# Attention into a mixture of experts on one core: other row order for the first w1 load, a longer hand-kept emission order

## The chip, the cores and the metric

One Trainium2 chip, one of its NeuronCores. The core has TensorE (PE), VectorE (DVE), ScalarE (ACT), GpSimd (POOL), a queue that only issues transfers (SP), and sixteen DMA engines. The metric is device time in microseconds of one launch; "before" was run three times. Times inside the launch are from one profiled execution and count from its first instruction.

## What is computed

Linear attention over 8 batches, 8 heads, 576 positions and 64 features, then a mixture of 8 experts over the 4608 tokens, every expert for every token, weighted by a matrix P that eight rounds of row and column normalising give.

```python
def _attn_ref(q, k, v):
    def phi(x):
        return np.where(x > 0, x, np.exp(x) - 1.0) + 1.0
    q_p, k_p = (phi(q), phi(k))
    kv = np.einsum('bhsd,bhse->bhde', k_p, v)
    z = np.sum(k_p, axis=2)
    num = np.einsum('bhsd,bhde->bhse', q_p, kv)
    den = np.einsum('bhsd,bhd->bhs', q_p, z)[..., None] + 1e-06
    return (num / den).astype(np.float32)

def _moe_ref(x, w_gate, w1, w2):           # x: 4608 x 512, w1: 8 x 512 x 1024, w2: 8 x 1024 x 512
    logits = x @ w_gate
    logits = logits - logits.max()
    P = np.exp(logits)
    for _ in range(8):
        P /= P.sum(1, keepdims=True) + 1e-09
        P /= P.sum(0, keepdims=True) + 1e-09
        P *= N / E
    for e in range(E):
        h = np.maximum(x @ w1[e], 0.0)
        ye = h @ w2[e]
        out += P[:, e:e + 1] * ye
```

## The kernel before

**Tiling.** The attention runs in 16 pairs (batch b, half g of the heads: two rows of two heads each). A pair loads k, q and v, makes phi(k) and phi(q) (exp on ACT, add-and-max and min on DVE), multiplies k with v (`kv_ps`), transposes q on TensorE (`att`), and forms denominators (`att`) and numerators (`num_ps`); the quotient goes to `xT`, the transposed input of the experts, in fp16. The experts run in units of 512 tokens, nine to an expert (g = 0 to 8). The first five units of expert 0 are plain products: layer 1 (`hq`, eight blocks of 128 hidden features) and layer 2 (`ye`). All later units but the very last use a seven-product scheme of Strassen's kind in both layers. It needs sums of blocks of w1 (tile W, four DVE instructions an expert), of w2 (tile T, four more), of x (kept in `xd` in HBM and loaded again as `xs` for each unit) and of h (tile S).

**How the order comes about.** Nothing is emitted in program order. Every piece of work is added to a plan (`_Plan.add`) with an engine, a cost in microseconds, dependencies and buffers, and gets a running number. `run` then emits the pieces one at a time: first those of the list `_FRONT`, in exactly its order, and after its end by its own rule, which takes whatever the cost figures say can start first. The engines execute what was emitted for them in that order, each its own queue, so the list fixes each queue. An entry is the number and a letter for the engine: p PE, a ACT, d DVE, g POOL, s SP, m a transfer's landing, n nothing (an allocation). The costs steer only the plan; no instruction depends on them.

**Numbers used in this document.** 2 to 47: small products that keep TensorE busy at the start. 48: k of pair 0 (on SP). 50, 52: q and v of pair 0 (POOL). 76, 78, 80: k, q, v of pair 1; 126, 128, 130 those of pair 2; 154, 156, 158 those of pair 3; 182, 184, 186 those of pair 4; 210, 212, 214 those of pair 5. 104 and 106: the two halves of w_gate. 109, 111, 114, 116: the four pieces of expert 0's w1, all on POOL; 120 and 123: the two halves of its w2. 600 to 603: layer 1 of the first unit for four blocks of hidden features, first half of the contraction (chunks 0 and 1 of four); 604, 606, 608, 610: the second half; 612 to 618 the other four blocks; 620 to 627 its layer 2. 985 and up: expert 1, 57 numbers to a unit, so 1156 to 1212 is its fourth. 1499 and 1501: the two loads of expert 2's w1; 1505: that of its w2; 1508 to 1511: the four sums W of expert 2; 1512 to 1515: the four sums T.

**The weight loads.** `load_w` allocates the tile and issues one POOL transfer for each entry of `pieces`; the fp32 weights are cast to fp16 on the way. The tile of w1 has 128 rows, four chunks and 1024 columns; row p of chunk c holds feature 256 * (p // 64) + 64 * c + p % 64 of x. `load_w1` with `parts=2` is used once, for expert 0. A product of the first half of the contraction depends on the first two pieces, one of the second half on the last two. All other w1 loads are two transfers of 64 rows and all four chunks. Eight POOL transfers can be in flight: the ninth is issued when the first has landed.

## Time and profile before

| | us |
|---|---|
| median of 3 runs | 979.66 (978.38 to 979.71) |
| the profiled execution | 979.93 |
| its span, first to last instruction | 978.2 |
| TensorE busy in the span | 956.6 |
| TensorE busy 0 to 10, 10 to 20, 20 to 30 | 8.67, 8.06, 2.15 |
| TensorE busy 30 to 40, 40 to 50 | 10.00, 9.99 |
| TensorE busy 260 to 280 | 17.07 |
| granted clock, 20 to 30 and 30 to 40 | 0.73, 0.76 |
| granted clock, 260 to 280; mean of the run | 0.91; 0.992 |

"Busy" counts an engine's instructions, overlaps once. Matmuls are pipelined: one of 512 columns is recorded as 0.379 us long, but the next starts 0.215 us after it, so a stretch of many is measured from start to start. The page's rows of busy shares have 40 slices of 24.5 us; the granted clock is TensorE's, as a share of full speed. In the lists of waits a row has the waiting engine, what it waited for, the total, how often, and the longest. A transfer's time to landing runs from its issue to its last mark.

Rows of the start, start time and length first (PE's small products left out):

```
7.82 1.16 ACT L422 ACTIVATE eq<-qin 128x1152 f16<-128x1152 f16 x1 [1.85 <-DMA qin<-in_q_dram]
9.97 0.85 POOL L289 DMA_DIRECT2D w<-in_moe_w_dram x1
19.04 0.75 DVE L473 TENSOR_TENSOR xT<-num_ps,rden 128x576 f16<-128x576 f32 x1
20.86 0.68 PE L414 MATMUL att<-ident,tq 128*128 128x128 f16 x9
29.69 1.04 PE L646 MATMUL hq<-xT,w 128*128 128x512 f16 x2 [7.00 <-DMA w<-in_moe_w_dram]
44.57 1.89 PE L874 MATMUL ye<-w,h 128*128 128x512 f16 x8
```

### The profile page before, as it was taken

Reading aid. Unit: us, or ns where it says so; the run is one execution under the profiler, and the core shown is the slowest. Engines: PE = TensorE matmul, PEld = TensorE weight load, DVE = VectorE, ACT = ScalarE, POOL = GpSimd, SP = SyncE. Lnnn points to the kernel's source line nnn. Section 1 sums busy time; section 2 is a strip of 40 time slices with the busy share of each in tenths; the row PEclk is TensorE's granted clock in tenths of the full one; section 3 lists DMA queues with packets and bytes.
Section 4 is the critical chain, followed back from the end, with each engine's and each line's share of the span. In section 5 each row is a group of like instructions: output and inputs, shape, how many; then the busy total and the mean of one; then the engine's idle time right before and its main releaser. Section 6 shows DMA issues by size and latency. Waiting matters only on the chain.

```text
span 978.2 us, 20907 instructions
## 1 busy us (share of the span) xinstructions
PE 956.6 (98%) x8480; PEld 796.8 (81%) x8480; DVE 775.9 (79%) x1489; ACT 569.8 (58%) x1012; POOL 147.1 (15%) x209
## 2 busy tenths in 40 slices
PE   7799999999899999999999999999999999999998
PEld 3365566678788888888888888888888888888886
DVE  6598988788778788878888788878888788877775
ACT  6598854466555555555555555555555555555553
POOL 6343200001212111121112111121112111111110
PEclk9799999999999999999999999999999999999999
DMA  9997927122625422272225422272224422236554
GB/s 196 221 228 176 183 93 233 37 76 76 125 76 122 116 76 77 76 162 77 77 76 125 114 77 76 77 162 76 76 77 123 116 76 76 77 91 168 163 163 108
DMA packets 49264, 112.51 MB, mean 115 GB/s; under 512 B 7952, under 2 KB 29200, under 8 KB 49168
## 3 DMA queue, kind: packets, MB, share of 16 engines
q1 hardware_dynamic: 21056, 75.57, 23.6%
q0 software_dynamic: 27712, 35.09, 19.6%
q8 instruction: 66, 1.08, 0.4%
q10 hardware_dynamic: 400, 0.52, 0.2%
q14 instruction: 30, 0.25, 0.1%
HBM read 119.69 MB, written 17.69 MB: 140 GB/s over the span
## 4 chain that ended last, share of the span: by engine, by line
PE 91%; DMA 4%; DVE 3%; ACT 1%; issue 1%; POOL 0%; DVEq 0%; ACTq 0%; POOLq 0%
PE ye L992 33%; PE hq L768 23%; PE att L768 12%; PE ye L874 6%; PE Zye L768 6%; PE Zye L992 5%; DMA w<-in_moe_w_dram 3%; PE hq L646 3%; PE att L445 1%; PE kv_ps L388 1%; PE num_ps L445 1%; DMA qin<-in_q_dram 1%; DVE xT L473 0%; PE att L414 0%; PE att L489 0%
## 5 line engine op out<-in xcount | busy, mean ns | idle before, releaser
L1006 DVE SCALAR_TENSOR_TENSOR acc<-ye,P_sb,acc 128x256 f32<-128x256 f32 x620 | 267.6, 479 | 125.2 <-PE ye L992 124.5
L768 PEld LDWEIGHTS <-W 128*128 128x128 f16 x2144 | 209.8, 98 | 34.0 <-issue 6.4
L992 PEld LDWEIGHTS <-S 128*128 128x128 f16 x1984 | 194.1, 98 | 22.4
L1016 POOL TENSOR_TENSOR acc<-acc,st 128x256 f32<-128x256 f32 x124 | 87.6, 726 | 720.2 <-ACT st L1013 720.2
L992 PE MATMUL ye<-T,S 128*128 128x256 f16 x1488 | 192.8, 273 | 0.0
L768 PEld LDWEIGHTS <-w 128*128 128x128 f16 x1608 | 157.6, 98 | 21.6 <-issue 0.5
L800 ACT ACTIVATE h<-hq 128x512 f16<-128x512 f32 x134 | 80.0, 597 | 142.3 <-PE hq L768 137.7
L992 PEld LDWEIGHTS <-h 128*128 128x128 f16 x1488 | 146.0, 98 | 17.5 <-issue 0.3
L768 PE MATMUL att<-xs,W 128*128 128x256 f16 x1008 | 151.6, 273 | 4.2 <-DVE h L803 3.8
L768 PE MATMUL hq<-xs,W 128*128 128x256 f16 x1008 | 151.2, 273 | 0.4 <-ACT Zye L780 0.4
L768 PE MATMUL hq<-xs,w 128*128 128x256 f16 x1008 | 141.2, 273 | 0.3 <-DVE h L803 0.3
L797 ACT ACTIVATE h<-Zye 128x512 f16<-128x512 f32 x134 | 80.1, 598 | 45.7 <-PE Zye L768 44.7
L1013 ACT ACTIVATE st<-Zye,P_sb 128x256 f32<-128x256 f32 x124 | 52.3, 471 | 75.7 <-PE Zye L992 75.5
L803 DVE CUSTOM_DVE_ANT_0 h<-att,s 128x512 f16<-128x512 f32 x126 | 86.5, 686 | 11.1 <-ACT s L787 10.2
L787 ACT COPY s<-hq 128x512 f32<-128x512 f32 x126 | 73.5, 583 | 35.9 <-PE hq L768 35.7
L965 DVE TENSOR_TENSOR S<-h 128x1024 f16<-128x1024 f16 x124 | 85.2, 687 | 11.3 <-ACT h L800 11.2
L780 ACT COPY Zye<-hq 128x512 f32<-128x512 f32 x134 | 77.8, 581 | 27.7 <-PE hq L768 27.6
L803 DVE CUSTOM_DVE_ANT_0 h<-hq,s 128x512 f16<-128x512 f32 x126 | 86.6, 687 | 3.2 <-PE hq L768 2.7
L794 ACT COPY s<-att 128x512 f32<-128x512 f32 x126 | 74.5, 591 | 5.3 <-PE att L768 3.3
L874 PE MATMUL ye<-w,h 128*128 128x512 f16 x312 | 77.1, 379 | 0.0
L768 PE MATMUL Zye<-xs,w 128*128 128x256 f16 x504 | 75.6, 273 | 0.0
L992 PE MATMUL ye<-T,h 128*128 128x256 f16 x496 | 65.2, 275 | 0.0
(104 smaller groups left out, 958.8 us busy)
## 6 DMA issues: line engine op xcount, KB each, us to landing
xs<-xd SPq DMA_DIRECT2D x63, 896.0 KB, 4.6
kin<-in_k_dram POOLq DMA_DIRECT2D x15, 576.0 KB, 6.5
out_dram<-acc SPq DMA_DIRECT2D x67, 128.0 KB, 2.4
w<-in_moe_w_dram POOLq DMA_DIRECT2D x16, 512.0 KB, 9.3
w<-in_moe_w_dram POOLq DMA_DIRECT2D x7, 1024.0 KB, 13.2
qin<-in_q_dram POOLq DMA_DIRECT2D x16, 288.0 KB, 7.1
vv<-in_v_dram POOLq DMA_DIRECT2D x16, 288.0 KB, 6.4
xd<-acc SPq DMA_DIRECT2D x5, 512.0 KB, 2.7
```

The costliest lines, as they stand in the source:

```text
L768: nc.tensor.matmul(dst[:, p, :], lhsT=lhs(p, c), rhs=rhs(c), start=(first and p == 0 and c == 0), stop=(c == 1), skip_group_check=True)
L780: nc.scalar.copy(out=Zt[1], in_=gX["tile"])
L787: nc.scalar.copy(out=gs2["tile"], in_=gX["tile"])
L794: nc.scalar.copy(out=gs5["tile"], in_=gR["tile"])
L797: nc.scalar.activation(out=hd(0, 0), in_=Zt[1], func=AF.Relu)
L800: nc.scalar.activation(out=hd(1, 0), in_=gX["tile"], func=AF.Relu)
L803: nc.vector._custom_dve(TENSOR_ADD_SAT, out=dst, in0=ps, in1=sb, s0=3.0e38, s1=0.0)
L874: nc.tensor.matmul(gy[tt]["tile"], lhsT=gh["tile"][:, f, ds(P * tt, P)], rhs=gw2["tile"][:, f, :], start=(f == 0), stop=(f == NFT - 1))
L965: nc.vector.tensor_tensor(out=Sx[:, i], in0=a0, in1=a1, op=op)
L992: nc.tensor.matmul(bank(g_)[:, s, :], lhsT=lhs(s, kk), rhs=rhs(kk), start=(new and s == 0 and kk == 0), stop=(kk == 3), skip_group_check=True)
L1006: nc.vector.scalar_tensor_tensor(out=dst(), in0=bank(g_)[:, s, :], scalar=P_sb[:, gg, e:e + 1], in1=dst(), op0=ALU.mult, op1=ALU.add)
L1016: nc.gpsimd.tensor_tensor(out=dst(), in0=dst(), in1=gst["tile"], op=ALU.add)
```

## The change

Three things change. Expert 0's w1 is still loaded in four pieces of 256 KB, but a piece was all 128 rows of one chunk, with the two groups of 64 rows as the outermost dimension on the HBM side; it becomes 64 rows of two chunks, with the 64 rows outermost on both sides. The first two pieces still hold chunks 0 and 1 and the last two chunks 2 and 3, so what depends on which pair stays. The list `_FRONT` is replaced: it had 1236 entries and ended in expert 1's sixth unit (1275p); it has 1465 and ends in expert 1's last unit. And two cost figures of the plan change: a piece's transfer from 1.4 to 1.6, and the add-and-max of phi(q) from 0.5 to 0.455.

```diff
-    1n 106g 107m 108n 119n 599n 48s 49m 2p 3p 50g 51m 4p 0g 5p 6p 52g 53m 7p 8p 76g 77m 9p 78g 79m 10p 11p 54a 55d
-    80g 81m 12p 13p 14p 15p 128g 129m 16p 56d 17p 18p 126g 127m 19p 20p 21p 61n 22p 62a 63d 130g 131m 23p 24p 25p 26p
-    27p 64d 156g 157m 28p 29p 30p 31p 32p 57n 109g 110m 58p 65p 59d 111g 112m 33p 60a 66d 34p 83d 67p 89n 82a 114g
...
-    1232p 1206d 1231a 1207p 1233a 1229a 1236p 1209d 1238p 1208d 1237a 1234p 1199a 1240p 1235a 1200g 1273p 1241d 1275p
+    1n 108n 119n 599n 109g 110m 48s 49m 2p 3p 50g 51m 4p 0g 5p 6p 52g 53m 7p 8p 76g 77m 9p 78g 79m 10p 11p 80g 81m
+    12p 13p 14p 15p 126g 127m 16p 54a 55d 17p 18p 128g 129m 19p 20p 21p 22p 130g 131m 23p 24p 25p 26p 27p 61n 111g
+    112m 62a 63d 28p 29p 56d 30p 31p 32p 33p 64d 34p 35p 36p 37p 57n 156g 157m 58p 65p 59a 82a 114g 115m 38p 66d 39p
...
+    104g 105m 122n 622p 200d 194a 617a 180p 201p 181d 620p 202a 178p 203p 125n 179d 244g 245m 621p 204a 623p 628d
+    106g 107m 217d 637p 639p 223n 216a 218d 270g 271m 224a 624p 225d 205a 226d 219n 272g 273m 220p 640d 638a 227p
...
+    549p 948p 550d 962p 949a 551d 912p 922d 635a 958p 913p 631a 959d 1498n 1499g 1500m 963a 988p 1501g 1502m 920d
...
+    1386n 1312g 1393p 1325d 1357a 1441s 1442m 1395p 1394a 1314g 1358d 1391p 1362p 1505g 1506m 1359d 1364p 1360d 1363a
...
+    1447a 1512d 1370a 1413p 1383d 1443n 1371g 1450p 1410d 1414a 1516s 1517m 1452p 1382d 1448p 1415d 1419p 1416d 1421p
+    1420a 1417d 1451a 1424p 1418d 1423d 1454p 1427a 1422d 1429p 1449a 1455d 1428g 1432p 1430d 1431d 1456p 1453d 1458p
...
-                ts_.append(add(("dma", (1.4 if nm == "w1" and len(pieces) > 1 else 2.75)), lambda _: None, deps=[ti],
+                ts_.append(add(("dma", (1.6 if nm == "w1" and len(pieces) > 1 else 2.75)), lambda _: None, deps=[ti],
...
-            return load_w(moe_w1, "w1", p_w1, [[((slice(None), c), PW * F * c, [[256 * F, 2], [F, PW], [1, F]])
-                                                for c in (2 * i, 2 * i + 1)] for i in range(2)], e, shape=[P, NDT, F], **kw)
+            return load_w(moe_w1, "w1", p_w1, [[((slice(64 * r, 64 * r + 64), slice(2 * i, 2 * i + 2)),
+                                                 256 * F * r + 2 * PW * F * i, [[F, PW], [PW * F, 2], [1, F]]) for r in range(2)]
+                                               for i in range(2)], e, shape=[P, NDT, F], **kw)
...
-        t3 = fadd(("dve", 0.5), f_qm, deps=[t0], use=[gin["q"], gtq], prio=pr)
+        t3 = fadd(("dve", 0.455), f_qm, deps=[t0], use=[gin["q"], gtq], prio=pr)
```

The queue of POOL at the start, before: 106, 50, (identity), 52, 76, 78, 80, 128, 126, 130, 156, 109, 111, 114, 116, 154, 158, 182, 186, 184, 120, 123, 210, 212, 214. After: 109, 50, (identity), 52, 76, 78, 80, 126, 128, 130, 111, 156, 114, 116, 154, 158, 182, 184, 186, 120, 123, 210, 212, 214, 240, 242, 268, 104, 244, 106.

## The prediction

> **What bounds the kernel now.** I read the page first, then busy time by stretch, then the waits of the two bad stretches, then the landings of the weight loads.

> ```profile
> span 978.2 us, 20907 instructions
> ...
> PE 956.6 (98%) x8480; PEld 796.8 (81%) x8480; DVE 775.9 (79%) x1489; ACT 569.8 (58%) x1012; POOL 147.1 (15%) x209
> ...
> PE   7799999999899999999999999999999999999998
> ...
> PEclk9799999999999999999999999999999999999999
> ```

> TensorE is the bound: 978.2 - 956.6 = 21.6 us idle in all. By stretch 11.1 of them lie before 30 us, 2.93 in 260 to 280, 4.27 at the end (drain of the last outputs, untouched) and 3.0 in four small places (0.76 in 100 to 120, 0.44 in 160 to 180, 0.87 in 200 to 220, 0.94 in 240 to 260). From 280 to 900 there is none. So a change can gain only before 30, around 265, and in crumbs. The stretches around both holes:

> ```profile
> 22.70:24.60 1.90, 0.00 (x0) 0.00 (x0) 0.83 (x2) 0.72 (x1) 0.00 (x0) 1.00 1.09 204
> 24.60:29.70 5.10, 0.01 (x1) 0.01 (x1) 0.00 (x0) 0.00 (x0) 0.00 (x0) 0.50 1.09 186
> 29.70:34.90 5.20, 5.20 (x15) 2.26 (x16) 0.99 (x2) 2.17 (x3) 3.65 (x5) 0.50 0.92 196
> ...
> 264.40:267.00 2.60, 0.03 (x1) 0.00 (x0) 2.60 (x6) 0.57 (x1) 0.00 (x0) 1.00 0.83 136
> ...
> 267.40:270.40 3.00, 3.00 (x15) 2.14 (x15) 1.39 (x3) 0.59 (x1) 0.00 (x0) 0.50 0.00 0
> ```

> Columns: PE, PE weight load, DVE, ACT, POOL busy, then granted clock. Each hole costs twice: the idle time, and then work at clock 0.50. The first: 7.0 us idle, then 5.20 us at half clock, 2.6 lost. The second: 2.92 idle, then 3.0 at half, 1.5 lost. Who is waited for, first stretch 0 to 40, then 250 to 270:

> ```profile
> POOL qin L353 <- DMA w<-in_moe_w_dram: 8.2, 1, 8.2
> ...
> PE hq L646 <- DMA w<-in_moe_w_dram: 7.0, 1, 7.0
> ```

> ```profile
> PE att L768 <- DVE h L803: 2.9, 1, 2.9
> DVE W L932 <- DMA w<-in_moe_w_dram: 2.5, 1, 2.5
> ```

> So both are weight loads: the first w1 (expert 0), and expert 2's w1, behind which DVE's queue stood. The landings of w to 60 us, and all DMA packets from 18 to 30:

> ```profile
> L289 POOL DMA_DIRECT2D w<-in_moe_w_dram x6: 762/784/852, 10.0 to 31.7; - x6
> ...
> DMA to landing us min/median/max: 11.1/17.5/19.7
> ```

> ```profile
> DMA packets 4604, 2.11 MB, mean 176 GB/s; under 512 B 3605, under 2 KB 3963, under 8 KB 4603
> ```

> The trace keeps sixteen landing marks for each POOL transfer, one per DMA engine. The first w1 piece (issued 9.97) has fourteen marks by 21.6 and two at 29.6; the next pieces have four, six and eight late marks (29.4 to 32.1). So each piece moves its data on **two engines**: 128 packets of 2 KB, 64 to an engine at 0.173 us, are 11.1 us, and 18.4 to 29.65 is 11.25. The 3605 short packets fit: 4 pieces x 14 idle engines x 64 empty packets = 3584. The old pieces have an outermost dimension of 2.

> **The change, part by part.** Estimates unless a row is named.

> 1. **Pieces with 64 rows outermost.** The nearest row is the later w1 loads, 64 rows outermost and 512 KB: expert 3's two land 314.86 and 317.39, all sixteen marks of each within 0.7 us, the same 0.173 us a packet. A 256 KB piece is 128/16 x 0.173 = 1.38 us; half of 2.53 is 1.27. I take 1.4.
> [...]

> 2. **The first piece goes to the head of POOL's queue, one w_gate half leaves it** (both halves now go out among the loads of pair 7, issued in some 0.8 us each). Every load behind is late by 8 x 0.173 minus the half's 16 x 0.025, so 1.0 us. Before, the first eight q/k/v loads on POOL land from 7.79 to 18.36, 1.51 apart. After: first q 8.8, the eighth (v of pair 2) 8.8 + 7 x 1.51 = 19.4, second w1 piece 20.8, q 22.3, pieces three and four 23.7 and 25.1, then k, v, k, q, v 26.6 to 32.6, and w2's halves (2.55 apart before) 35.2 and 37.7. Before they landed at 42.0 and 44.56: DMA leads by 6.8.

> 3. **TensorE in front.** The first layer-1 product (600) needs the second piece (20.8), the first xT (its second evict ended 19.80, so 20.8) and the transpose ahead of it on PE (q of pair 2, moved behind its k, lands 17.9; exp and min 2.2, transpose to about 21.2). It starts at 21.3 instead of 29.69: **8.4**. What is late next: with full clock, 600 to 603 and four attention products take 2.7 us, to 24.0, then the second half of the contraction waits for 25.1; later v of pair 3 (28.1) and w2. The first w2 product ran at 44.57 and can now run at 35.5, the first with w2's second half at 46.82 and now 38.1, kv of pair 5 at 51.47 and now 42.6 (its v lands 42.2): leads 9.1, 8.7, 8.9. The half clock saves 2.6 and the waits for DMA take most of that back. From there TensorE is busy through as before, with ACT and DVE (8.3 to 10 of 10) moving along, and POOL is held by free buffers, not by DMA. Bounds: DMA's lead 6.8 less one clock step of 3.4 us at half (1.7), so 5.1; above, 8.4 + 2.6 = 11.0. I take **8.5**.

> 4. **Does the clock fall in the new front?** It fell 1.9 us into the idle time at 22.7, and 2.6 us into the one at 264.4; the waits that I expect in 21 to 36 are 1 to 2 us each. So one step is possible; the 8.5 holds none, the lower bound one.
> [...]

> 5. **The list now holds expert 2's loads.** Before, the written list ended at 1275 and held neither of 1499, 1501 (w1) and 1505 (w2): POOL issued them together at 251.05, 251.67 and 252.27, they landed 256.77, 262.55 and 267.2, and the four combinations of w1 stood in DVE's queue already: 2.47 of waiting and 4 x 0.68 of work came between the evicts, 5.2 us, and TensorE was out for 2.92 of them, so DVE can be some 2.3 us late for nothing. Now w1's two stand at the first products of expert 1 (186 in the old count), the combinations 1508 to 1511 some 45 to 80 us of TensorE work behind: no wait. Behind the loads on POOL stand only accumulations, which idled 10.0 us before the one at 245.16. w2's load is tighter. From 1505 to T's first combination 1512 I count 16 products, ten of four matmuls (0.44) and six of eight (0.87), 9.6 us, while the seven w2 loads of 1024 KB landed in 13.2 us in the median, behind w1's loads; alone, 1024 packets at 0.098 on 16 engines are 6.3, an x load issued just ahead (1441) 2.4, and the start 1.4 to 2.7: 10 to 12 us. So DVE waits 0.5 to 2.5 us there, works 0.68, and TensorE pays up to 0.9. Gain 2.92 + 1.5 - 0.4 = **4.0**; bounds 0 (the like hole again) and 5.4 (the 0.94 of 240 to 260 too).

> 6. **The other moves of the list** (attention, expert 0 and 1). The rows show 3.0 us of small idle time to win, and nothing shows which places the new order fills or opens: -3 to +3. I take +0.3, near nothing. The two cost figures that change (1.4 to 1.6 and 0.5 to 0.455) emit nothing; they only feed the plan behind the list, after 1458.

> **Sum.** 8.5 + 4.0 + 0.3 = 12.8. Span 978.2 - 12.8 = 965.4; the execution stood 1.7 above its span (979.93), so 967.1, and 0.27 above the median shown, so **966.9**.

> **Rivals.**
> - *DMA or the clock eats the front.* One clock step, or transfers spaced wider than 1.51, bring item 3 to its lower end: 979.66 - (5.1 + 4.0 + 0.3) = 970.3. For: DMA is above nine tenths to 45 us. Against: fewer bytes wait on two engines. 0.13.
> - *The second hole moves* to T's first combination: w2 takes 13 us as its sisters, DVE stands 3.4 us, the next combinations crowd behind, clock falls: 966.9 + 4.0 = 970.9. For: the count of item 5. Against: one combination, not four, stands there. 0.13.
> - *Half-rate pieces.* If 64 rows of a tile took in data at half rate, four pieces cost 5.5 more, w2 lands at 40.7, the lead at its first product falls from 9.1 to 3.6, and the time is 966.9 + 5.5 = 972.4. The later loads' 0.173 us speak against it. 0.03. [...]
> - *The order gains more*: the crumbs go too, 966.9 - 2.7 = 964.2. 0.10.
> - *Slower.* PE, ACT and DVE run in the order written. If the new list, on wrong durations, leaves PE behind a late DVE evict in expert 1's units as at 264.4, each costs 2.92 + 1.5 = 4.4; the point is three of nine units: 3 x 4.4 = 13.2 eats all (980.1), four give 984.5. For: the new list orders all nine one by one, where the old one left the last four to the plan. Against: DVE has a fifth of its time free in the steady units (79.6 busy of 100 us from 400 on), and there the same products run with no idle time at all. 0.03.
> - *The pieces still go on two engines*, because the tile side decides: 64 is outermost there too, so hardly; then the second piece still lands at 19.4 + 11.1 = 30.5, and items 5 and 6 are left, 979.66 - 4.3 = 975.4. 0.02.

> **How the numbers follow.** My forecast has 0.56, own range 964.5 to 969.3 (terms +-2.4). The range takes in the half-gain cases and the better order, 962.5 to 972.5; left out are the slower case, the two-engine case and some of the edges, 0.15 to 0.2. A measurement of this kernel tells about 0.2% (2 us) from no change. Faster by more: 0.96 (all but the slower case and a part of the two-engine one); within 0.01; slower 0.03.

> **What would show it.** Right: the w1 pieces' landing falls from 18 us to under 12, with far fewer short packets before 30 us; the wait of hq on w gone or under 1 us, first hq at 20.5 to 22.5; PEclk full in 20 to 35; w2's first product near 35.5; no DVE wait on w and no PE idle near 265, a DVE wait under 2.5 us at the end of expert 1; the rest of the units at the old pace. Wrong: first hq later than 25 (item 1 or 2), a clock of 0.5 in front (item 4), a PE wait above 1 us on a DVE evict in expert 1 (item 5 or 6), or a lead in front that shrinks between 50 and 130 us, which would mean that ACT or DVE, not TensorE, sets the pace of the attention stage.

## The result, and the profile after

| | before | after |
|---|---|---|
| median, us | 978.38 (977.47 to 979.71) | 968.91 (966.96 to 972.92) |
| ratio, 95% interval | | 0.9906 (0.988 to 0.9931) |
| profiled execution, its span | 979.93, 978.2 | 968.34, 966.5 |

Five executions of each, side by side on one chip. In the experiments one execution of the kernel with two entries moved took 2021 us, with TensorE at half pace (four products of 256 columns at 400 us in 1.16 us, 0.60 with the warm-ups spread), and is left out of its figures.

The page after:

```profile
span 966.5 us, 20909 instructions
...
PE 954.4 (99%) x8480; PEld 795.6 (82%) x8480; DVE 774.7 (80%) x1484; ACT 571.8 (59%) x1017; POOL 145.8 (15%) x209
...
PE   8999999999999999999999999999999999999998
...
PEclk9999999999999999999999999999999999999999
```

TensorE's idle time fell from 21.6 to 12.1 us (966.5 - 954.4), and the row of the granted clock no longer has a low slice. Of the 11.7 us of span, 9.5 are idle time and 2.2 busy time; the busy time is the balance of less work at half clock later and more of it at the very start, as shown below. The stretches, with columns as before (PE, PE weight load, DVE, ACT, POOL busy; clock; DMA share; GB/s):

```profile
22.70:24.60 1.90, 1.53 (x18) 0.91 (x14) 1.81 (x4) 1.87 (x3) 1.51 (x2) 1.00 1.06 347
24.60:29.70 5.10, 4.92 (x33) 2.84 (x33) 4.60 (x8) 4.36 (x6) 2.49 (x3) 1.00 1.16 268
29.70:34.90 5.20, 4.98 (x39) 2.39 (x37) 4.92 (x9) 5.20 (x8) 2.65 (x4) 1.00 1.24 209
262.00:266.00 4.00, 4.00 (x39) 3.59 (x38) 3.77 (x8) 0.78 (x3) 0.00 (x0) 1.00 0.02 4
278.00:288.00 10.00, 9.39 (x86) 8.11 (x84) 8.30 (x17) 5.28 (x11) 0.85 (x1) 1.00 0.55 137
```

The first hole was 22.7 to 29.7; now TensorE is 12.2 - 11.43 = 0.77 us short of busy from 22.7 to 34.9, at full clock. The second hole (264.4 to 267.4) is gone. Behind it, up to the drain of the last outputs, TensorE idles 0.61 us in 278 to 288 and 0.33 near 950. All DMA packets from 18 to 30, and then the w loads to 60 us:

```profile
DMA packets 1756, 3.07 MB, mean 256 GB/s; under 512 B 136, under 2 KB 1154, under 8 KB 1755
```

```profile
DMA to landing us min/median/max: 5.2/11.6/13.0
```

Short packets fell from 3605 to 136 in that stretch, and over the run from 7952 to 4368: the difference is 3584 = 4 pieces x 14 idle engines x 64, to the packet. The longest time to landing fell from 19.7 to 13.0. But TensorE's own start was later (start, length):

```profile
4.72 7.24 PE L575 MATMUL yw<-warm 128*128 128x512 f16 x28
11.89 0.92 PE L401 MATMUL kv_ps<-vv,t 64*128 64x192 f16 x18
...
23.70 0.59 PE L659 MATMUL hq<-xT,w 128*128 128x512 f16 x2
...
36.44 0.81 PE L887 MATMUL ye<-w,h 128*128 128x512 f16 x3
```

The first kv ran at 9.50 before, and its v had landed at 9.83 in this run. It stood behind 36 small warm-up products (31 before), 13 of them at half clock up to 6.83 (0.43 apart, then 0.216); before, 7 were, and the spacing changed at 4.23. So the first layer-1 product runs at 23.70 (29.69 before) and the first product on w2 at 36.44 (44.57).

**The lead.** To say where time came from, I count TensorE's products in the order in which they ran and compare the moments at which two kernels have started the same number. The lead is the moment in the profiled execution of before minus that of the other kernel. Four points, by the time at which before stood there: 74 us (front over), 252 (ahead of the second hole), 283 (behind it), 339 (expert 2 under way).

| kernel | 74 | 252 | 283 | 339 |
|---|---|---|---|---|
| after | 7.7 | 7.6 | 12.7 | 11.7 |
| after, again | 8.4 | 6.9 | 11.9 | 9.1 |
| new pieces, old list | 8.7 | 8.7 | 7.3 | 7.3 |
| new list, old pieces | -1.7 | -2.9 | 2.1 | 1.2 |
| after, warm-ups spread | 8.7 | 8.0 | 13.0 | 12.1 |
| new pieces, old list, expert 2's loads early | 8.2 | 8.2 | 12.2 | 12.2 |
| spread, two entries moved, first piece later | 9.3 | 9.5 | 14.6 | 13.6 |
| the same, two edits more | 9.1 | 9.4 | 14.4 | 13.5 |
| after, pieces of 62 + 2 rows | -6.3 | -7.1 | -2.1 | -4.9 |
| after, pieces of 60 + 4 rows | 8.3 | 6.8 | 11.8 | 10.9 |

From 339 to the end no lead moves by more than 0.1, so what the plan makes behind the list, the two cost figures included, shows nothing. Counted by columns instead of products, the leads at 74 of the kernels with the new list come out 0.2 lower, the other figures the same: the orders mix long and short products differently there.

All leads are against one execution of before, and that one took 979.93, 1.5 above the median of its five. So a lead of 11.6 at the end stands beside 9.5 between the medians. Its half clock at the start ended at 4.23, earlier than in any other trace here, but its mean granted clock is low, 0.992: of the 39 executions of before in the experiments, the 20 with 0.996 or 0.997 took 976.3 to 979.5, the 13 with 0.992 to 0.994 took 978.9 to 981.4. The highest of the five of after, 972.92, has 0.997 where the others have 0.999 and 1.0; there is no trace of it, so where its clock fell isn't known.

### The profile page after: what moved, and what is told of

Same layout as the page of the kernel before. It is cut to its first block, busy times and chain, and to the rows that moved or that the text cites. A ratio compares the mean times of both kernels' runs of the same rounds, so it can differ in the third digit from the quotient of the medians.

```text
span 966.5 us, 20909 instructions
## 1 busy us (share of the span) xinstructions
PE 954.4 (99%) x8480; PEld 795.6 (82%) x8480; DVE 774.7 (80%) x1484; ACT 571.8 (59%) x1017; POOL 145.8 (15%) x209
## 2 busy tenths in 40 slices
DMA packets 45680, 112.50 MB, mean 116 GB/s; under 512 B 4368, under 2 KB 25616, under 8 KB 45584
## 4 chain that ended last, share of the span: by engine, by line
PE 92%; DVE 3%; ACT 2%; issue 1%; DMA 1%; POOL 0%; DVEq 0%; POOLq 0%; ACTq 0%
PE ye L1005 32%; PE hq L781 23%; PE att L781 12%; PE ye L887 6%; PE Zye L781 6%; PE Zye L1005 5%; PE hq L659 3%; PE yw L575 1%; DVE h L816 1%; DVE acc L1019 1%; PE kv_ps L401 1%; PE att L458 1%; DVE S L978 1%; DMA kin<-in_k_dram 1%; PE num_ps L458 1%
## 5 line engine op out<-in xcount | busy, mean ns | idle before, releaser
L781 PEld LDWEIGHTS <-w 128*128 128x128 f16 x1608 | 157.3, 98 | 21.2 <-issue 1.0
L800 ACT COPY s<-hq 128x512 f32<-128x512 f32 x126 | 73.5, 583 | 34.9 <-PE hq L781 34.8
## 6 DMA issues: line engine op xcount, KB each, us to landing
w<-in_moe_w_dram POOLq DMA_DIRECT2D x7, 1024.0 KB, 13.2
```

The source lines that it names most:

```text
L781: nc.tensor.matmul(dst[:, p, :], lhsT=lhs(p, c), rhs=rhs(c), start=(first and p == 0 and c == 0), stop=(c == 1), skip_group_check=True)
L800: nc.scalar.copy(out=gs2["tile"], in_=gX["tile"])
```

## The experiments

Ten kernels, in three groups, each of five rounds beside the kernel before (medians 978.67, 978.34 and 979.41).

**The changed kernel once more**, without an edit.

> The changed kernel once more. Theory: its first kv product starts when the small products ahead of it on TensorE have run, and those run at half clock until a clock window ends that has no fixed place in the run; so the full clock comes at another time than the 6.9 us of the first profile, and the first kv product moves with it, between 10.2 and 12.5 us, and the first layer-1 product between 22 and 24. Rival: the first kv product is at 11.9 again whatever the clock does, because data sets it. Time 967 to 970 in both.

Measured: 969.84 (968.97 to 970.94), ratio 0.9904 (0.9888 to 0.9921). In this run the warm-ups left half clock at 5.46 and kv of pair 0 ran at 11.17, the first product on w2 at 35.72: 0.7 earlier than in the run above, with the same code: data doesn't set the first kv, the warm-ups do. It then lost time in two places. On TensorE:

```profile
81.65 0.41 PE L458 MATMUL num_ps<-qpT,kvz 128*128 128x288 f16 x2 [1.77 <-ACT kvz L326]
```

```profile
79.80 1.16 ACT L376 ACTIVATE ek<-kin 128x1152 f16<-128x1152 f32 x1 [2.36 <-DMA kin<-in_k_dram]
80.87 0.73 ACT L326 CAST kvz<-kv_ps 64x256 f16<-64x256 f32 x2
```

```profile
284.64 0.69 DVE L957 TENSOR_TENSOR T<-w 128x1024 f16<-128x1024 f16 x1 [1.83 <-DMA w<-in_moe_w_dram]
```

```profile
286.38 0.60 PE L781 MATMUL att<-xs,W 128*128 128x256 f16 x4 [2.20 <-DVE h L816]
```

The brackets give the idle time ahead of the instruction and its releaser. At 80 us ACT stood 2.36 us for a k that had not landed, with the copy of kvz that TensorE needed next in its queue. At 284 DVE stood for expert 2's w2, which took 12.4 us to land here (272.26 to 284.61) and 9.6 in the run above (271.53 to 281.13), where DVE arrived just behind it. TensorE lost 1.77 and 2.51 (the 2.20, and 0.31 just ahead of it). Both losses were 0.34 and 0.61 in the first run: the changed kernel has two waits whose size is a matter of the run. The six traces that have w2's load in this place lost 0.9 of lead behind 283 four times and 2.8 twice.

**The new pieces alone**: the kernel before, with the new `load_w1`.

```diff
-  [[((slice(None), c), PW * F * c, [[256 * F, 2], [F, PW], [1, F]])
-    for c in (2 * i, 2 * i + 1)] for i in range(2)]
+  [[((slice(64 * r, 64 * r + 64), slice(2 * i, 2 * i + 2)),
+     256 * F * r + 2 * PW * F * i, [[F, PW], [PW * F, 2], [1, F]]) for r in range(2)] for i in range(2)]
```

> The kernel before, with the new row order of the first w1 pieces and nothing else. Theory (the old pieces ran on two engines, and that made the first hole): the pieces land 1.4 us apart, at about 21.2 to 25.5, first layer-1 product at 21.6 to 23 in place of 29.7, no half clock there, lead 7 to 8.5 us after the front; the hole at 265 stays with its 4.2. Time 970 to 972. Rival (the new list closed the first hole, the pieces are hidden): within 2 us of the kernel before.

Measured: 971.92 (968.45 to 973.22), ratio 0.9923 (0.9905 to 0.9941). The lead is 8.7 behind the front and stays there to 252: the row order by itself gives all of the front, no less than the whole change (7.7 and 8.4). The second hole is as it was, 2.83 us idle:

```profile
PE att L769 <- DVE h L804: 2.8, 1, 2.8
...
DVE W L933 <- DMA w<-in_moe_w_dram: 2.4, 1, 2.4
```

In the profiled execution two windows of half clock fell on it instead of one (257.74 to 264.57, 6.83 us):

```profile
260.00:270.00 10.00, 10.00 (x74) 8.03 (x72) 6.79 (x14) 3.42 (x8) 1.41 (x2) 0.77 0.27 92
```

TensorE is busy all the time here and does 0.77 of its work. That is the fall of the lead from 8.7 to 7.3, and a matter of this execution: the fastest of the six took 968.45, at a mean granted clock of 1.0.

**The new list alone**: the changed kernel, with the old `load_w1` (the diff above, reversed).

> The changed kernel with the old row order of the four pieces. Theory (two engines): the first piece, now at the head, holds two engines for 11 us from about 4 us on, so the first q, v and k get their last marks only after 15 us, and the second piece ends at 30 or later; first layer-1 product at 31 or later, half clock, front lead below 0; only the second hole's 4.2 and the crumbs' 1.3 are left. Time 974 to 982. Rival (the list does it): first layer-1 product before 26, time 971 or less.

Measured: 979.78 (976.5 to 981.41), ratio 1.0009 (0.9996 to 1.0022): no difference that can be told.

```profile
POOL vv L365 <- DMA w<-in_moe_w_dram: 11.9, 2, 8.4
...
PE kv_ps L400 <- DMA vv<-in_v_dram: 7.6, 1, 7.6
```

The list puts the first piece at the head of POOL's queue. With two engines its last marks come at 16.27, and the loads behind it land only after that: q of pair 0 at 17.54, its v at 18.97 (8.42 and 9.83 in the changed kernel), and TensorE waits 7.6 us for that v. The lead is -1.7 behind the front; the second hole gives its 5.0 all the same. So the two parts of the change aren't independent: this list is only of use with pieces that spread.

**Warm-ups spread**: eleven warm-up products, 33 to 43, moved behind the products that follow them. (44 to 47 change place in the list, but not in TensorE's own queue.)

```diff
- ... 31p 32p 33p 64d 34p 35p 36p 37p 57n 156g 157m 58p 65p 59a ... 38p ... 67p ... 69p ... 95p ... 97p
+ ... 31p 32p 64d 57n 156g 157m 58p 65p 33p 34p 35p 36p 37p 59a ... 67p 38p 39p 40p ... 69p 41p 42p ... 95p 44p 45p 46p ... 97p 47p
```

> The changed kernel with 31 instead of 36 of the small products ahead of the first kv product, as in the kernel before; the other five stand behind its first transpose, and the rest spread over the next attention products. Theory (the small products at the head of TensorE's queue cost the front some 1 to 2 us): the first kv product starts at 10.0 to 11, the first layer-1 product at 22.0 to 22.8 in place of 23.7, the lead stays and the time is 1 to 1.4 us less than the changed kernel's. Rival 1 (DMA sets the front): the first w2 product stays at 36.4, no gain. Rival 2: the clock falls to half for one window in the gaps, 1.7 us slower.

Measured: 968.27 (967.92 to 968.96), ratio 0.9889 (0.9871 to 0.9907). kv of pair 0 at 10.87 although the clock came as late as in the first run (the spacing changes at 6.85), and the lead in front 8.7. So 1.0 of the front's shortfall was the products put ahead of the first kv. The medians show less: this one is 0.6 and 1.6 below the two of the changed kernel, and its executions lie within the spread of the first.

**Expert 2's loads early, in the old list.**

```diff
- ... 1004p 1003a 631d 964p 1005a ... 1014p ... 1275p
+ ... 1004p 1498n 1499g 1500m 1501g 1502m 1003a 631d 964p 1005a 1503n ... 1014p 1504n ... 1275p 1505g 1506m 1507n
```

> The kernel before, with the new first w1 pieces, and in its old list only expert 2's three weight loads put in early (w1 behind product 1004, w2 at the end of the list); every other entry stays where it was. Theory: the second hole was late loads, nothing else. Then no wait of DVE on w near 258 to 268, no TensorE hole at 265, lead 8.7 in front plus 4.2 there: 978.7 - 12.9 = 965.8, in 964.5 to 967.5, some 5 to 6 below the run with the new pieces alone (971.9). Rival: the hole was made by the order of expert 1's evicts, which only the searched list mends; then a hole of 2 us or more is still there between 255 and 285, and the time is 970 to 972.

Measured: 967.79 (967.52 to 968.39), ratio 0.989 (0.9873 to 0.9907); 0.3 above the range named, 4.1 below the new pieces alone. The old hole would stand near 256 to 259 here; TensorE has no idle time in these windows:

```profile
250.00:260.00 10.00, 10.00 (x94) 8.96 (x92) 7.87 (x17) 5.79 (x12) 1.51 (x2) 1.00 0.42 100
260.00:270.00 10.00, 10.00 (x94) 8.96 (x93) 8.29 (x16) 5.62 (x11) 1.41 (x2) 1.00 0.22 86
270.00:280.00 10.00, 10.00 (x94) 8.97 (x92) 7.92 (x16) 5.33 (x11) 1.41 (x2) 1.00 0.25 93
```

DVE works its four W earlier, without a wait:

```profile
243.14 0.68 DVE L932 TENSOR_TENSOR W<-w 128x1024 f16<-128x1024 f16 x1
...
244.34 0.68 DVE L932 TENSOR_TENSOR W<-W,w 128x1024 f16<-128x1024 f16 x1
...
245.33 0.68 DVE L932 TENSOR_TENSOR W<-w 128x1024 f16<-128x1024 f16 x1
...
246.32 0.68 DVE L932 TENSOR_TENSOR W<-w,W 128x1024 f16<-128x1024 f16 x1
```

An idle time of 1.54 us stands at 244.6 (TensorE waits for an ACT copy behind four scalings of acc). Before has two smaller ones there:

```profile
253.23 0.60 PE L768 MATMUL hq<-xs,W 128*128 128x256 f16 x4 [0.44 <-ACT Zye L780]
...
254.23 0.60 PE L768 MATMUL att<-xs,W 128*128 128x256 f16 x4 [0.40 <-ACT s L794]
```

So the lead falls by 0.6, from 8.2 to 7.6, and then grows to 12.2: in the old order the hole alone was worth 4.5. What it says is the more: three loads put earlier in the **old** list, with the new pieces, are at 967.79, below both medians of the kernel with the whole new list (968.91 and 969.84). What else the new list changes gained nothing that shows, and it brought the two waits.

**Two entries moved**, on top of the spread warm-ups: w2 of expert 2 is issued earlier, and one exp stands later on ACT.

```diff
- ... 446a ... 365a ... 366a ... 349a ... 1257g ... 1314g 1358d 1391p 1362p 1505g 1506m
+ ... 365a ... 366a ... 349a 446a ... 1257g 1505g 1506m 1507n ... 1314g 1358d 1391p 1362p
```

> The kernel with warm-up products spread, and two entries moved: w2 of expert 2 is issued behind the accumulation 1257 instead of behind 1314, and the exponential of k of pair 6's second head set stands behind three later evicts on ACT instead of ahead of them. Theory: the losses at 80 us (0.3 to 1.8) and at 280 to 287 (1.3 to 2.8) are those two waits for a landing. Then the issue of w2 is near 256 and its landing near 268, DVE's T does not wait, no product near 80 idles over 0.3, the lead behind 300 is 12.8 to 13.5, and the time 966.0 to 967.5 (967.0), with the spread of its runs under 1. Rival: the idle time at 281 to 283 is the order of DVE's evicts and not the landing; then the lead falls by 1 there all the same, and the time stays at 967.5 to 968.5.

Measured: 966.21 to 967.25 in four executions, ratio 0.9878 (0.986 to 0.9895); all four are below the lowest of the warm-ups spread alone (967.92). The next kernel has both edits, and its trace shows them.

**The first piece later**: on top of that, 109 behind the load 130.

```diff
- 1n 108n 119n 599n 109g 110m 48s 49m ... 130g 131m 23p
+ 1n 108n 119n 599n 48s 49m ... 130g 131m 109g 110m 23p
```

> As the kernel with the two entries moved, and the first w1 piece goes out behind the first four q, k, v loads of POOL instead of ahead of them. Theory: at the head of the queue the first piece costs those loads 1.0 us each, and they are what the first product kv of pair 0 needs once the warm-ups no longer stand in its way. Then q0 lands at 7.5 (8.5 before), v0 at 8.9, kv of pair 0 starts at 9.9 to 10.3, and with the second piece unchanged at 19.8 the lead in front grows by 0 to 0.6: 966.5. Rival: the first layer-1 product needs both first pieces and waits for the last of them in any order, so nothing moves behind 22 us, and the time is that of the kernel with the two entries moved.

Measured: 966.91 (966.28 to 967.13), ratio 0.9878 (0.9863 to 0.9893).

```profile
79.05 1.16 ACT L375 ACTIVATE ek<-kin 128x1152 f16<-128x1152 f32 x1 [0.57 <-DMA kin<-in_k_dram]
80.23 0.60 ACT L663 ACTIVATE h<-hq 128x512 f16<-128x512 f32 x1
```

```profile
253.72 0.93 POOL L300 DMA_DIRECT2D w<-in_moe_w_dram  x1
```

```profile
281.82 0.60 PE L780 MATMUL att<-xs,W 128*128 128x256 f16 x4 [0.30 <-DVE h L815]
```

ACT still waits 0.57 for that k, but nothing that TensorE needs stands behind it, and no product near 80 idles. w2 is issued at 253.72 and lands at 265.7; T at 280.07 waits for nothing. Yet 0.31 and 0.30 of idle time stay at 279.6 and 281.8, and the lead falls by 0.9 there: of the loss at T, the part that the landing makes (up to 1.9 more) is cured, the other part is the order. The theory of the kernel with two entries moved and its rival each had half of it. Of the first piece: q of pair 0 lands at 6.88 (8.42 after), its v at 8.73 (9.83), kv starts at 9.79. The lead in front is 9.3, 0.6 above the spread warm-ups alone, but the clock came 2.1 us earlier in this run (4.72), which makes some 1.0 by itself; this doesn't separate the two. The time is that of the kernel without this edit, as the rival had it: the later first piece shows no gain.

**Pieces of 62 and 2 rows.** What makes two engines of sixteen? The traces so far have two cases of the outermost dimension: the old pieces with 2 groups, on two engines, and the new ones with 64 rows, whose sixteen marks lie within 0.5 to 1.8 us. Two more numbers can be tried without touching a byte or the order: cut each piece of 64 rows in two. I expected two engines for 62 rows and fifteen for 60, which no run before these two showed, and for 62 rows the time of the new list with the old pieces (979.8), in 977 to 982.

```diff
-  nc.gpsimd.dma_start(out=g["tile"][sl], in_=AP(tensor=ten.tensor, offset=e * DM * F + off, ap=ap))
+  cuts = [(0, 62), (62, 64)] if nm == "w1" and len(pieces) > 1 else [(0, ap[0][1])]
+  for a, b in cuts:
+      s2 = (slice(sl[0].start + a, sl[0].start + b), *sl[1:]) if len(cuts) > 1 else sl
+      nc.gpsimd.dma_start(out=g["tile"][s2], in_=AP(tensor=ten.tensor,
+                          offset=e * DM * F + off + a * ap[0][0], ap=[[ap[0][0], b - a], *ap[1:]]))
```

> The changed kernel with each of its four first w1 pieces cut into two transfers, of 62 rows and of 2 rows; all bytes, and the order, as in the changed kernel. [...] Rival: the rows are dealt over all sixteen engines whatever their number, so each transfer lands within 1.5 us, and the time is that of the changed kernel plus four short issues, 968.5 to 971.5.

Measured: 984.69 (981.6 to 986.43), ratio 1.0057 (1.0039 to 1.0076): slower than before.

**Pieces of 60 and 4 rows**, the control: the same edit with (0, 60), (60, 64).

> As the kernel with 62 and 2 rows to a piece, but 60 and 4. [...] Rival: it is the cutting into two transfers that made the run with 62 rows slow (984.7); then this run is slow too, 982 to 986.

Measured: 968.92 (968.2 to 970.99), ratio 0.9903 (0.9886 to 0.9921): the changed kernel's time. The sixteen landing marks of the first piece's larger transfer, issued at 1.66 in both (us):

```
62 rows  4.9 5.0 5.0 5.0 5.0 5.1 5.1 5.1 5.1 5.2 5.2 5.2 5.3 5.3 15.6 16.1
60 rows  4.9 5.7 5.8 5.8 5.8 5.8 5.8 5.8 5.8 5.9 5.9 5.9 5.9 5.9  5.9  6.0
```

Fourteen early and two late, 11 us apart, against one early and fifteen within 0.3. The first 20 us, 62 rows and then 60:

```profile
0.00:20.00 20.00, 11.06 (x54) 5.25 (x54) 4.70 (x10) 3.61 (x3) 11.88 (x20) 0.88 0.83 165
```

```profile
0.00:20.00 20.00, 16.42 (x107) 7.91 (x108) 10.53 (x20) 10.64 (x13) 14.15 (x26) 1.00 1.00 209
```

And all packets of the run, in the same order:

```profile
DMA packets 49328, 112.51 MB, mean 114 GB/s; under 512 B 8016, under 2 KB 29264, under 8 KB 49232
```

```profile
DMA packets 45872, 112.50 MB, mean 116 GB/s; under 512 B 4560, under 2 KB 25808, under 8 KB 45776
```

The short packets can be counted out from the marks. The changed kernel has 4368. Its POOL issues 76 transfers, and the trace has 1216 packets of 4 B on its queue, sixteen to a transfer; so four transfers more bring 64. With 62 rows, two engines have 62 packets each and fourteen as many short ones: 4 x 14 x 62 = 3472; the 2-row transfers, if they are on two engines as well, 4 x 14 x 2 = 112: 8016 in all. With 60 rows on fifteen engines one engine has 8 short ones and, if 4 rows go on four engines, twelve have two: 4 x (8 + 24) = 128: 4560. Both are met to the packet. Sixty rows or 62 of 64 in the larger transfer are the difference between 969 and 985 us. With 62 the first layer-1 product ran at 32.59 (23.70 in the changed kernel); the time is 2.7 above the range that I gave. Against the list with the old pieces, the last pieces land 3.0 later (39.08 for 36.12) and w2's halves 2.6 (48.33 and 50.84), one more window at half clock falls at 39 to 42.5, and the place at T took 2.8 of lead in this run.

**Two edits more**, on the kernel with the first piece later: five more warm-ups behind the first kv, and T behind two evicts.

```diff
- ... 28p 29p 56d 30p 31p 32p 64d 57n 156g 157m 58p 65p 33p ... 1512d 1370a ... 1383d ... 1410d ... 1382d 1448p 1415d
+ ... 56d 64d 57n 156g 157m 58p 65p 28p 29p 30p 31p 32p 33p ... 1370a ... 1383d ... 1410d ... 1382d 1512d 1448p 1415d
```

> The kernel with the warm-ups spread, the two entries moved and the first w1 piece behind four loads, and two edits more: five more warm-up products go behind the transpose of q of pair 0 (26 instead of 31 are left ahead of the first kv), and DVE's first combination of T stands behind the two evicts and the h that followed it. Theory: kv of pair 0 then starts when its v has landed, 8.9 to 9.7 instead of 9.79, and the product that waited 0.30 at 281.8 for h no longer waits, while the 0.31 ahead of it (a bank that DVE empties) stays; lead behind 300 13.9 to 14.8, time 966.1 (965.3 to 966.9). Rival: the front is bound by the second w1 piece and the weight loads behind it, so that an earlier kv is given back by 45 us, and the time stays at 966.5 to 967.2.

Measured: 966.48 (966.25 to 966.86), ratio 0.9874 (0.9857 to 0.9891). A miss: the lead is no better (13.5 against 13.6) and the median is within the other's spread. DVE, then TensorE:

```profile
280.86 0.48 DVE L1018 SCALAR_TENSOR_TENSOR acc<-ye,P_sb,acc 128x256 f32<-128x256 f32 x1 [0.53 <-PE ye L1004]
281.26 0.68 DVE L815 CUSTOM_DVE_ANT_0 h<-att,s 128x512 f16<-128x512 f32 x1
```

```profile
281.99 0.60 PE L780 MATMUL att<-xs,W 128*128 128x256 f16 x4 [0.30 <-DVE h L815]
```

With T out of the way DVE now idles 0.53 for the product of TensorE that it evicts next, and h comes as late as before. TensorE and DVE wait for each other in this place; T was not the cause of this 0.30. The front is no clean test of the moved warm-ups: the half clock ended at 6.42 here and at 4.72 in the run before it, and the second piece landed at 21.23 for 20.53. The first kv came 0.21 earlier (9.58), the first layer-1 product 0.40 later (22.01).

## Why the prediction was right, and where it was off

The direction, the two mechanisms and the range were right; the time came out 2.0 above the number (968.91 against 966.9). The number stood on a median of 979.66 from three runs. Beside it, five runs of before had 978.38, and 978.38 less the sum of 12.8 is 965.6: the gain between the medians is 9.5, and 8.8 when the kernel ran again (978.67 to 969.84). In the two profiled executions the lead is 11.6 at the end. By the steps:

- **Item 1, pieces at 1.4 us.** Right. The third and fourth land 1.37 apart (23.37 and 24.75), the marks of each piece lie within 0.5 to 1.8, and the short packets fell by the 3584 that I had counted. A piece of 262144 bytes in 1.37 us is 191 GB/s; the rival of half-rate pieces, with some 1.4 us more for each, did not show.
- **Item 2, the landings.** Right within 1.2: first q 8.42 (8.8 said), second piece 19.66 (20.8), w2's halves 34.14 and 36.64 (35.2 and 37.7). The price of the head of the queue, 1.0, is about what the later first piece gave back: v of pair 0 at 8.73 for 9.83.
- **Item 3, the front, 8.5.** Two errors of opposite sign, so that it came out near is in part luck: 7.7 and 8.4 in the two runs of the changed kernel. The first layer-1 product ran 6.0 and 6.7 earlier than before (23.70 and 22.99), not 8.4, and missed the sign that I had named, 20.5 to 22.5. The chain I wrote for the first product began with loads and evicts and left out what stood at TensorE's own queue head: 36 warm-ups, five more than before and at half clock for 1.2 to 2.6 us longer. 2.6 us of half clock cost 1.3, five products cost 1.1; together 2.4, and kv of pair 0 was 2.39 later than before. On the other side I let waits for DMA take back most of the 2.6 that before lost at half clock behind its first product; here 1.7 of it was kept, in both runs; DMA's lead at w2 was 7.9 (42.01 to 34.14), not 6.8. With fewer warm-ups ahead of the first kv the lead was 8.7, and with the old list too.
- **Item 4, the clock.** No half clock in the front, behind the first warm-ups, in any trace with pieces that spread (1.00 from 20 to 40 us in those of the new pieces alone and of 60 rows), so the sum's choice was right. Where the pieces were on two engines the clock fell again (15.96 to 22.79 in the run with the list alone).
- **Item 5, expert 2's loads, 4.0.** The mechanism was right and shown by itself. From 252 to 283 the lead grew by 5.0; 1.2 of that came by 256, from the two small waits of before near 254 that I had only in the upper bound, so the hole gave 3.9 in the new order and 4.5 in the old one, where 4.4 was said. The price at T, 0.4 with a bound of 0.9, was too low: 0.9 in the first run and 2.8 in the second. The landing of 10 to 12 us was right (9.6 and 12.4), DVE's wait was right (none, and 1.83), but I charged TensorE for a part of the wait only, and not for the evicts that DVE and TensorE owe each other there with no wait for a landing at all (0.6 idle or more in every trace with the new list). The second rival was half of this: the wait at T happens in some executions, with no half clock behind it.
- **Item 6, the other moves, +0.3.** Between 74 and 252 us the lead moved by -0.1 and -1.5, inside the bounds; the list as a whole shows no gain here. The loss at 80 us is one entry on ACT ahead of a landing.
- **The rival of two engines** had its price wrong: 975.4 said, 979.8 measured. It left out that the first piece would then hold up the whole q, k, v queue behind it, which item 2 had worked out only for a piece that spreads.

## What to carry to other kernels

## What the runs showed of the hardware

**The half clock at the start ended at no fixed moment.** The warm-ups, always 46 and alike at the start, left half clock between 4.23 and 6.85 us after the first instruction (4.23 in before, 6.83 and 5.46 in the two runs of the changed kernel, 6.85 with the warm-ups spread, 4.72 with the first piece later, 6.42 with two edits more), and the start of the real work moved with it by 0.7 us between the two runs of one kernel (11.89 and 11.17). The stretches of full and half clock behind it, up to 270 us, were multiples of 3.41 us in the trace of before: 20.48, 10.24, 232.11 and 3.41 (6, 3, 68 and 1); the half clock of the new list alone, 15.96 to 22.79, and that of the new pieces alone, 257.74 to 264.57, were 6.83 (2). So part of the spread of these times is made in the first 7 us.

**Idle engines get packets too.** POOL's queue had 4800 packets of 4 B before and 1216 after. The 3584 more are, to the packet, one for every data packet of a busy engine (64 to a piece) on each of the fourteen without data, for the four old pieces. No run here prices them by themselves.

**One load's landing varied by over a quarter.** Expert 2's w2, the same 1024 KB with the same neighbours, took 9.6 and 12.4 us in the two runs of the changed kernel. An instruction placed to arrive with a landing is placed on that spread.
